# The second tile's M4, M7 and M3 go by quarter blocks, on one core

## The chip, the core and the metric

The kernel runs on one core of a Trainium2 chip. The metric is the device time of one execution in microseconds, and less is better. Five engines of the core matter here: TensorE (PE), whose weight loads are listed apart as PEld, VectorE (DVE), ScalarE (ACT), GpSimd (POOL) and SyncE (SP), which only issues DMAs. Each works through its own instruction queue in the order in which it was written, and semaphores make one wait for another.

## The reference

```python
def _attn_ref(q, k, v, proj):              # 4 batches, 8 heads, 768 rows, 64 wide
    mask = q_bucket[:, :, :, None] == k_bucket[:, :, None, :]   # hash buckets from the signs of q@proj, k@proj
    scores = np.where(mask, scale * np.matmul(q, k.transpose(0, 1, 3, 2)), -1e9)
    ...
    return np.matmul(attn, v)

def _moe_ref(x, w_in, w_out):              # x 3072 x 512, w_in 512 x 2048, w_out 2048 x 512
    h = x @ w_in
    sp = np.maximum(h, 0.0) + np.log1p(np.exp(-np.abs(h)))
    g = h * erf(sp)
    return (g @ w_out).astype(np.float32)
```

The attention's output, 3072 rows of 512, is the `x` of the feed-forward part. Everything is in float32. The change is in the feed-forward part alone.

## The kernel before

**The two halves.** Attention comes first and takes the span up to about 312 us. `feed_forward` (from L1341 on) then works on six tiles of 512 rows each, t = 0 to 5.

**Two products of a tile.** A tile's first product, `x @ w_in`, and its second, `g @ w_out`, are each done by Strassen's scheme in the form of Winograd: a 2 x 2 block product costs seven block products (M1 to M7, and P1 to P7 on the first side) in place of eight, and sums of blocks in between. For tiles 1 to 5 the first side goes two levels deep: each of the seven P is again seven quarter products Q1 to Q7 (`small`, L1672), 49 in all, called the chain of the tile. A quarter product is four matmuls of 128 rows by 128 columns. The profile shows a float32 matmul as two records, so a chain has 392.

**The second side** takes the gated hidden values in four quarters a11, a21, a12, a22 (`quarter`). `presum_g` (L1908) makes the sums S.0 (s1 = a21 + a22), S.1 (s2 = s1 - a11), S.2 and S.3 of them on DVE, each in two halves fl = 0, 1. M6 multiplies s2 and M5 s1; M1, M2, M3, M4 and M7 multiply quarters. A block product done whole (`project`, L1989) is eight products of two matmuls of 256 columns: 16 matmuls, 32 records. Done by quarter blocks (`project_small`, L2145) it is seven quarter products of four matmuls of 128 columns: 28 matmuls, 56 records. That form needs four sums of its left operand on DVE (`presum_a`, L2120, words A4.0 to A4.3 for M4), and three sums of its weights, which POOL makes with four instructions (`presum_b`, L2069). The sums of weights lie in one buffer, key `("b",)`, part of it in a slot of the ring of chain weights. The first tile that uses them also writes them to DRAM (`keep_b`, L2079, POOL), and every later tile loads them from there (`load_b`, L2083, SP). Four ACT copies (L2158) and two DVE adds (L2163, L2167) take the results out of PSUM; `combine` (L2030 and L2032) joins the seven products.

**Slots.** While PE does the chain of tile t + 1, it also does the second side of tile t; the two are interleaved product by product. Below, slot n is the stretch in which the chain of tile n runs. In slot 1, tile 0's second side is done, in slot 2 tile 1's, and so on; tile 5's comes behind slot 5. `script(t)` (L1913) writes down the order of tile t's second side in words. Tile 0 has a script of its own, tile 1 (`t < HALVES`) goes through all seven products whole, and tiles 2 to 4 mix: M6 with the pieces of M4, M5 with those of M7, and then M3 in pieces. Tile 5 mixes M2 with M4 and M6 with M7, and does M3 whole.

**Gating.** Between the two sides stands the gate, for each quarter in two halves: six ACT passes over 128 x 1024 (L1821, L1829 four times, L1846) and three DVE passes (L1835 twice, L1850).

**The order.** Each piece of work is an `op` with an engine, an assumed cost, what it reads and writes, and a rank. `by_need` (L187) plays the whole feed-forward part with these costs several times, and the order that it finds is the order in which the instructions are written into the queues. On PE the lowest rank goes first among what is ready by the plan, on the other engines what is due first. A chain's product has rank t + (place / 49). A second-side product has rank `at` + (place / 56), with `at` = t + 1 + LAG, so LAG says by how much the second side stands behind the chain. The ring of chain weights has two places: `load_wi` (L1641, on SP) loads the weights of one P, 1792 KB, as soon as the P before the last has been done.

Of the kernel before, what the change touches and what calls it, by code (L numbers as in the profile page):

```python
# [294 lines left out]
def kernel(  # L295
# [34 lines left out]
    small = ctx.enter_context(tc.tile_pool(name="small", bufs=3))  # L330
# [1010 lines left out]
    def feed_forward(pools, check, late):  # L1341
        again = late is None
        work = pools["work"]
        NTILE = NT // T
# [24 lines left out]
        def op(name, engine, cost, rank, fn, args, reads=(), writes=(), after=(), **more):  # L1369

            needs = set(after)
            for x in tuple(reads) + tuple(writes):
                if x in wrote:
                    needs.add(wrote[x])
            for x in writes:
                needs |= read.get(x, set())
            for x in reads:
                read.setdefault(x, set()).add(name)
            for x in writes:
                wrote[x] = name  # L1380
                read[x] = set()
            needs.discard(name)
            more.setdefault("late", dict(PE=0.4, DVE=0.3, ACT=0.3, POOL=0.35, SP=0.3)[engine])
            ops.append(
                Op(name, engine, cost, rank, lambda: fn(*args), after=tuple(sorted(needs, key=str)), **more)
            )
# [526 lines left out]
        def script(t):  # L1913
            if t == 0 and not again:
                first = " ".join(f"{name}.{k}" for ks in (range(4), range(4, 8)) for name in ("M1", "M2", "M4") for k in ks)
                return first + " C.0 C.1 C.4 S.0 S.1 S.2 S.3 M6 C.2 M7 C.3 C.9 M5 C.5 M3 C.7"
            if t < HALVES and not again:
                return "M1 C.11 S.0 S.1 S.2 M2 C.12 S.3 M4 C.4 M6 C.2 M7 C.3 C.9 M5 C.5 M3 C.7"
# [35 lines left out]
            )  # L1954


        HALVES = 2

        OPERAND = dict(M1=0, M2=2, M3=2, M4=3, M5="s1", M6="s2", M7=1)

# [205 lines left out]
            u = into_of(name)[:, 1, :]  # L2166
            nc.vector.tensor_tensor(out=u, in0=flat(bank_of(t, "Z" + name[1]))[:, P:TH], in1=u, op=ALU.add)  # L2167

        LAG, LAST_LAG = 0.04, 0.16

        def second_ops(t):

            at = t + 1 + (LAG if t != NTILE - 2 else LAST_LAG)

            def presums(k, rank):
                for fl in range(2):
# [62 lines left out]
            def whole(name):  # L2239
                return tuple(("wt", WHOLE_KEY[name], fl) for fl in range(2)) if name in WHOLE_KEY else (("w22",),)  # L2240

            def blocks_of(name):
                if t == HALVES and not again:
                    for k in range(4):
                        op(
                            ("presum_b", name, k),
                            "POOL",
                            1.26,
                            (1, at + 0.1, k),
                            presum_b,  # L2250
                            (name, k),
                            port=True,
                            reads=whole(name),
                            writes=(("b",), ("w", "P4", 0), ("w", "P4", 1)) + (whole(name) if k == 0 else ()),
                        )
                    op(
                        ("keep_b", name),
                        "POOL",
                        1.5,
                        (1, at + 0.1, 4),  # L2260
                        keep_b,
                        (name,),
                        reads=(("b",),),
                        writes=(("mb", name),),
                        late=5.0,
                        far=True,
                    )
                    return

                apart = name == "M4" and t < NTILE - 1  # L2270
                op(
                    ("load_b", t, name),
                    "SP",
                    0.1,
                    (1, at + now[0] / 56, 0),
                    load_b,
                    (name,),
                    reads=(("mb", name),),
                    writes=(("b",),),
                    after=(("small", t + 1, 0, "Q4"),) if apart else (),  # L2280
                    late=7.0,
                    far=True,
                )
# [58 lines left out]
            def take_word(word):  # L2342
# [6 lines left out]
                elif kind == "N1":  # L2349
                    now[0] += 0.5  # L2350
                    products("M1", int(rest), t + 1)
                    now[0] += 0.5
                elif kind == "S":
                    k = int(rest)
                    presums(k, (0.05, 0.1, 0.2, 0.4)[k])
                elif kind == "C":
                    combines(int(rest))
                elif kind[0] == "L":
                    blocks_of("M" + kind[1])
                elif kind == "T":  # L2360
                    op(
                        ("turn", t),
                        "POOL",
                        1.26,
                        (1, at + 0.1),
                        presum_b,
                        ("M3", 0),
                        port=True,
                        writes=(("w22",),),
                    )  # L2370
                elif kind[0] == "A":
                    sums("M" + kind[1], int(rest))
                elif kind[0] == "R":
                    take("M" + kind[1], rest)
                else:
                    now[0] += 0.5
                    half(kind, rest)
                    now[0] += 0.5
# [50 lines left out]
        for t in range(1, NTILE + 1):  # L2429
            rest = second_ops(t - 1)  # L2430
            if t < NTILE:
                x_ops(t)
                chain_ops(t)
                for q in (0, 2, 3, 1):
                    gate_ops(t, q)
            rest()
        if late:
            for k, (engine, cost, name) in enumerate(
# [9 lines left out]
                    after=((name, k // 2), ("late", k - 1)),  # L2448
# [66 lines left out]
    with ExitStack() as rooms:  # L2515
        with tc.manual_schedule():
            late = attention()
            pools = open_pools(rooms)
            ending = feed_forward(pools, (measured, judge, decide, ask), late)
        with tc.If(bound["again"] == 0, preferred_fallthrough_block=False) as arms:  # L2520
            with tc.manual_schedule():
                for each in ending:
                    each.emit()
        with arms.Else():
            general(pools)
            feed_forward(pools, None, None)
# [53 lines left out]
```

## Time and profile before

| | |
|---|---|
| Time, median of 3 runs (lowest to highest) | 874.19 us (872.89 to 875.64) |
| The profiled execution | 874.26 us, of which 872.5 us are its span |
| Chains of tiles 1 to 5 begin at | 364.9, 454.5, 546.6, 638.5 and 728.9 us; the last ends at 813.6 |
| Weight sums on POOL (L2069) | M4's begin at 498.7, M7's at 590.0, M3's at 614.3 us |
| Tile 1's M1, M2, M4, M6, M7, M5 and M3 begin at | 458.9, 473.0, 485.2, 498.4, 512.5, 524.7 and 538.8 us |
| M6 of tile 2 and the first piece of its M4 begin at | 577.4 and 579.1 us |

Times within the span are counted from its first instruction. The page gives busy time for each engine. Since matmuls are pipelined, the time from the start of one record to the start of the next says more of PE's rate than the mean duration of one does. A wait is shown in square brackets behind an instruction: how long its engine sat idle before it, and whose semaphore came last.

### The profile page before, as it was taken

How to read it: one execution, taken by the hardware profiler on the slowest of the kernel's cores; microseconds unless marked ns; L12 is line 12 of the kernel's file. 1: busy time of each engine (PE TensorE's matmuls, PEld its weight loads, DVE VectorE, ACT ScalarE, POOL GpSimd, SP SyncE). 2: the span in 40 equal slices, each digit the busy share in tenths (PEclk: the TensorE clock that was granted, in tenths of full speed). 3: DMA queues.
4: the chain of work that ended last, by engine and by line, in shares of the span. 5: the costliest groups of instructions: out<-in, count | busy, mean ns of one | idle time of the engine just before them, and what ended most of it. 6: DMA issues, size and time to landing. Idle time of an engine off the chain costs nothing.

```text
span 872.5 us, 15270 instructions
## 1 busy us (share of the span) xinstructions
PE 864.5 (99%) x5992; PEld 670.8 (77%) x5992; DVE 748.8 (86%) x926; ACT 638.2 (73%) x895; POOL 209.8 (24%) x274
## 2 busy tenths in 40 slices
PE   9999999999999999999999999999999999999997
PEld 5444544444454468998999999999999999999996
DVE  5999999999899799789996877799779978898982
ACT  6888888888888757786589467845777586758840
POOL 1112121111111000425241453235732433110000
PEclk9999999999999999999999999999999999999999
DMA  9567766556662255685564647555586657655211
GB/s 228 149 190 194 222 187 182 171 150 172 181 177 96 87 173 204 234 315 188 192 182 145 229 154 209 179 168 184 146 271 224 206 158 219 215 177 162 98 61 41
DMA packets 99825, 155.30 MB, mean 178 GB/s; under 512 B 35182, under 2 KB 48542, under 8 KB 98848
## 3 DMA queue, kind: packets, MB, share of 16 engines
q1 hardware_dynamic: 90112, 120.96, 44.8%
q0 software_dynamic: 9184, 32.81, 12.3%
q8 instruction: 49, 0.80, 0.4%
q10 hardware_dynamic: 448, 0.46, 0.2%
q14 instruction: 32, 0.26, 0.1%
HBM read 119.50 MB, written 29.46 MB: 171 GB/s over the span
## 4 chain that ended last, share of the span: by engine, by line
PE 94%; DMA 3%; DVE 1%; issue 1%; ACT 1%; DVEq 0%
PE M L1672 23%; PE M L1989 22%; PE st L687 18%; PE av L772 14%; PE M L1433 6%; PE M L2145 5%; DMA w_in_sb<-wi_P 3%; PE X L2145 2%; PE bits L975 1%; PE bits L816 1%; PE warm L936 1%; DVE area L1908 0%; PE X L1989 0%; DVE h L1850 0%; DVE e L1835 0%
## 5 line engine op out<-in xcount | busy, mean ns | idle before, releaser
L687 PE MATMUL st<-q,k 64*128 64x384 f32 x768 | 155.1, 483 | 0.0
L1672 PE MATMUL M<-area,w_in_sb 128*128 128x128 f32 x1120 | 146.7, 275 | 1.8 <-DVE h L1702 1.2
L1672 PEld LDWEIGHTS M<-area,w_in_sb 128*128 128x128 f32 x1120 | 142.2, 192 | 6.9 <-DVE h L1702 1.6
L1835 DVE SCALAR_TENSOR_TENSOR e<-w,e 128x1024 f32<-128x1024 f32 x96 | 125.0, 1302 | 20.0 <-ACT w L1829 19.5
L1702 DVE TENSOR_TENSOR h<-M,h 128x512 f32<-128x512 f32 x161 | 108.4, 686 | 33.5 <-PE M L1672 29.7
L1989 PE MATMUL M<-w_out_sb,h 128*128 128x256 f32 x528 | 130.8, 380 | 1.7 <-issue 1.7
L1829 ACT ACTIVATE w<-h,cq 128x1024 f32<-128x1024 f32 x96 | 109.7, 1142 | 22.0 <-DVE e L1835 22.0
L1829 ACT ACTIVATE w<-w,cq 128x1024 f32<-128x1024 f32 x96 | 110.3, 1149 | 1.8
L1672 PEld LDWEIGHTS M<-i,w_in_sb 128*128 128x128 f32 x840 | 107.9, 192 | 3.9
L1672 PE MATMUL M<-i,w_in_sb 128*128 128x128 f32 x840 | 110.4, 275 | 0.0
L1989 PEld LDWEIGHTS M<-w_out_sb,h 128*128 128x128 f32 x528 | 92.8, 191 | 10.5 <-issue 2.0
L1989 PE MATMUL M<-wt,area 128*128 128x256 f32 x384 | 96.3, 380 | 0.0
L687 PEld LDWEIGHTS st<-q,k 64*128 64x128 f32 x768 | 68.5, 187 | 35.7 <-issue 34.4
L760 DVE TENSOR_TENSOR area<-area 128x1536 f32<-128x1536 f32 (+1 forms) x46 | 79.2, 1721 | 6.9 <-ACT area L714 5.7
L1654 POOL TENSOR_TENSOR i<-area,i 128x128 f32<-128x128 f32 x70 | 46.3, 681 | 139.6 <-PE M L1672 138.6
L1821 ACT ACTIVATE e<-h,cq 128x1024 f32<-128x1024 f32 x48 | 54.9, 1144 | 33.8 <-DVE h L1702 22.0
L714 ACT ACTIVATE e_even<-st 128x768 f32<-128x768 f32 x96 | 73.9, 820 | 0.4 <-PE st L687 0.3
L714 ACT ACTIVATE area<-st 128x768 f32<-128x768 f32 x90 | 72.7, 811 | 0.3 <-PE st L687 0.3
L1989 PEld LDWEIGHTS M<-wt,area 128*128 128x128 f32 x384 | 66.9, 191 | 6.0 <-DVE area L1908 0.2
L1850 DVE TENSOR_TENSOR h<-h,e 128x1024 f32<-128x1024 f32 x48 | 61.0, 1271 | 9.8 <-ACT e L1846 9.8
L772 PE MATMUL av<-e_even,v 128*64 128x385 f32 x384 | 65.7, 490 | 0.0
L687 PE MATMUL st<-both 64*128 64x384 bf16 x384 | 63.0, 323 | 0.2 <-ACT e_even L714 0.2
(187 smaller groups left out, 1323.9 us busy)
## 6 DMA issues: line engine op xcount, KB each, us to landing
w_in_sb<-wi_P SPq DMA_DIRECT2D x35, 1792.0 KB
raw<-in_w_out_dram POOLq DMA_DIRECT2D x16, 512.0 KB, 4.1
raw<-in_w_in_dram POOLq DMA_DIRECT2D x14, 512.0 KB, 5.5
v<-in_v_dram SPq DMA_DIRECT2D x32, 192.0 KB
out_dram<-area SPq DMA_DIRECT2D x23, 256.0 KB
q<-in_qkT_dram SPq DMA_DIRECT2D x30, 192.0 KB
k<-in_qkT_dram SPq DMA_DIRECT2D x30, 192.0 KB
r<-rd SPq DMA_DIRECT2D x30, 192.0 KB
```

What stands on the lines that cost most here:

```text
L687: nc.tensor.matmul(out=st[:, ab, 0:HS], lhsT=d["k" + src][rows, keys], rhs=d["q" + src][rows, cols], start=(part == 0), stop=(part == 1),)
L714: nc.scalar.activation(out=e[:, :, 0:HS], in_=st[:, :, 0:HS], func=AF.Exp, scale=scale)
L760: nc.vector.tensor_tensor(out=into, in0=one, in1=two, op=ALU.add)
L772: nc.tensor.matmul(out=d["av", half][rows, 0:w], lhsT=d["v"][:, g * GC + c, rows], rhs=e[:, ab, 0:w], start=(g == 0 and c == 0), stop=(g = ...
L1672: nc.tensor.matmul(out=out_[:, c, :], lhsT=ring[:, W_AT[q], n % 2, c * P : (c + 1) * P], rhs=x, start=((q in ("Q1", "Q5") or q == "Q2" and ...
L1702: nc.vector.tensor_tensor(out=out_, in0=bank_, in1=one, op=ALU.add)
L1821: nc.scalar.activation(out=s, in_=unit(t, q, fl), func=AF.Sigmoid, bias=cq[:, 0:1])
L1829: nc.scalar.activation(out=st["q", t, q, fl, j], in_=f, func=func, scale=scale, bias=cq[:, column : column + 1])
L1835: nc.vector.scalar_tensor_tensor(out=s, in0=st.pop(("q", t, q, fl, j)), scalar=GATE_S[j][1], in1=s, op0=ALU.add, op1=ALU.mult,)
L1850: nc.vector.tensor_tensor(out=h, in0=h, in1=st.pop(("s", t, q, fl)), op=ALU.mult)
L1989: nc.tensor.matmul(out=where[:, sub, :], lhsT=a[:, j // G, j % G, sub * P : (sub + 1) * P], rhs=b[:, j, :], start=first, stop=end, skip_gr ...
L2145: nc.tensor.matmul(out=where[:, n * P : n * P + P], lhsT=a[:, j, :], rhs=b[:, j, :], start=(q in ("Q1", "Q2") and j == 0), stop=(q in ("Q4 ...
```

## The change

`HALVES` falls from 2 to 1, so tile 1 is no longer done whole: it takes the mixed script of tiles 2 to 4, and M4, M7 and M3 of tile 1 go by quarter blocks. `blocks_of` tests `t == HALVES`, so the weight sums of M4, M7 and M3 are now made and kept in the slot of tile 1's second side, and tile 2 loads them from DRAM, as tiles 3 to 5 do. The sums get one more wait: none of them is made before the first quarter product of the next tile's chain (`("small", t + 1, 0, "Q1")`). Two ranks are moved: the second side of tile 0 stands behind its chain by 0.05 and no longer 0.04, that of tile 4 by 0.13 and no longer 0.16.

```diff
-        HALVES = 2
+        HALVES = 1
...
-        LAG, LAST_LAG = 0.04, 0.16
+        LAG, LAST_LAG = 0.04, 0.13
...
-            at = t + 1 + (LAG if t != NTILE - 2 else LAST_LAG)
+            at = t + 1 + (0.05 if not t else LAG if t != NTILE - 2 else LAST_LAG)
...
                             (name, k),
                             port=True,
                             reads=whole(name),
+                            after=(("small", t + 1, 0, "Q1"),),
                             writes=(("b",), ("w", "P4", 0), ("w", "P4", 1)) + (whole(name) if k == 0 else ()),
```

## The prediction

> **What bounds the kernel now.** I read the page's first two parts and its chain first.
>
> ```profile
> PE 864.5 (99%) x5992; PEld 670.8 (77%) x5992; DVE 748.8 (86%) x926; ACT 638.2 (73%) x895; POOL 209.8 (24%) x274
> ...
> PEclk9999999999999999999999999999999999999999
> ...
> PE 94%; DMA 3%; DVE 1%; issue 1%; ACT 1%; DVEq 0%
> ```
>
> PE is busy throughout, at the full granted clock, and 94% of the chain that ended last is PE. Then I read the windows, cut so that each of the first five holds the 392 records of one chain: slots 1 to 5 and what is behind them.
>
> ```profile
> core 0: us, PE busy (x) PEld busy (x) DVE busy (x) ACT busy (x) POOL busy (x), PEclk, DMA share, GB/s
> 364.90:454.50 89.60, 88.40 (x597) 82.61 (x597) 79.74 (x86) 67.77 (x73) 35.72 (x43) 1.00 0.67 227
> 454.50:546.60 92.10, 92.10 (x617) 86.34 (x616) 70.36 (x73) 63.78 (x72) 34.07 (x41) 1.00 0.57 183
> 546.60:638.50 91.90, 91.90 (x697) 88.37 (x697) 75.59 (x85) 58.15 (x73) 43.39 (x47) 1.00 0.57 181
> 638.50:728.90 90.40, 90.34 (x690) 86.86 (x688) 79.24 (x94) 64.67 (x80) 30.16 (x33) 1.00 0.64 209
> 728.90:813.60 84.70, 84.21 (x632) 80.72 (x633) 72.38 (x88) 65.94 (x78) 12.83 (x20) 1.00 0.58 184
> ```
>
> In slot 2, where the change acts, PE is never idle. So a microsecond less of PE work there is a microsecond less of time, as long as no wait takes its place. The waits of PE that there are stand in its timeline; these three hold nearly all of its idle time behind the first chain's start:
>
> ```profile
> 410.29 1.16 PE L1672 MATMUL M<-area,w_in_sb 128*128 128x128 f32 x8 [1.20 <-DVE h L1702]
> 740.23 1.16 PE L1672 MATMUL M<-area,w_in_sb 128*128 128x128 f32 x8 [0.45 <-DMA w_in_sb<-wi_P]
> 861.88 3.69 PE L1989 MATMUL M<-w_out_sb,h 128*128 128x256 f32 x16 [1.66 <-issue]
> ```
>
> The last is the branch ahead of tile 5's M3, which stays.
>
> **The products.** The price of both forms comes from starts, since matmuls overlap. Whole (from the chain of waits, eight records, in alternation with chain products as in slot 2) and by quarters (PE's timeline, the first and the last of ten rows, all of L1672 or L2145 with 128 columns, 88 records between the two starts):
>
> ```profile
> 742.28 1.73 PE M L1989 x8
> 744.01 1.78 PE M L1672 x16
> ```
>
> ```profile
> 717.07 1.06 PE L2145 MATMUL M<-w_out_sb,h 128*128 128x128 f32 x8
> ...
> 726.89 1.06 PE L2145 MATMUL X<-w_out_sb,h 128*128 128x128 f32 x8
> ```
>
> Whole: 1.73 / 8 = 0.216 us a record, times 32 = 6.92 us. By quarters: (726.89 - 717.07) / 88 = 0.1116, times 56 = 6.25 us. One block product falls by 0.67 us and three by **2.0 us**, with 0.05 either way for rounding. Slot 4, which has three block products by quarters, is 90.4 us against 92.1 for slot 2: 1.7, which fits, as the slots are not cut at the same place of the second side.
>
> **What DVE gets in slot 2.** The rows are those of slot 3, where tile 2 already goes by quarters (DVE busy in L2120, L2163, L2167, then L2032 in slots 2 and 4):
>
> ```profile
> 546.60:638.50 91.90, 11.26 (x12) 1.00 0.57 181
> ...
> 546.60:638.50 91.90, 1.25 (x3) 1.00 0.57 181
> ...
> 638.50:728.90 90.40, 0.85 (x3) 1.00 0.64 209
> ...
> 454.50:546.60 92.10, 2.07 (x3) 1.00 0.57 183
> 638.50:728.90 90.40, 5.61 (x7) 1.00 0.64 209
> ```
>
> Twelve sums of operands cost 11.3 us and six adds out of PSUM 1.25 + 0.85 = 2.1. `combine` has five adds in the mixed script (C.13, C.9, C.5, C.6, C.14) and had three: two more of 5.61 / 7 = 0.8, that is 1.6. Together 15.0 us, so DVE in slot 2 goes from 70.4 to about 85.4 of 90.1 us: 95%. Slot 1 has 79.7 of 89.6 (89%) and the one PE wait on DVE; slot 4 has 79.2 of 90.4 (88%) and none. So I cost these 15 us at nothing, hidden by PE's 90, but this cover is thin; a rival below says what it costs when it gives out.
>
> **POOL and DMA.** Of the twelve weight sums, M4's four are in slot 2 already (498.7). M7's and M3's eight move there from slot 3:
>
> ```profile
> 546.60:638.50 91.90, 13.89 (x8) 1.00 0.57 181
> ```
>
> POOL (L2069 in slot 3) gets 13.9 us more in slot 2, 34.1 to 48 of 90, and as much less in slot 3. M7's sums can only overwrite the buffer when M4's pieces have been read; POOL stands still meanwhile, and the chain's own small sums (L1654) and x sums (L453) are queued behind. In slot 3 this happened and PE, the one who waits for them, did not stand:
>
> ```profile
> 591.35 2.14 POOL L2069 TENSOR_TENSOR w_in_sb<-w_out_sb 128x512 f32<-128x512 f32 x1
> 597.14 1.28 POOL L2069 TENSOR_TENSOR w_in_sb<-w_out_sb,w_in_sb 128x512 f32<-128x512 f32 x1 [3.66 <-PE M L2145]
> ```
>
> The same distances hold in slot 2: cost nothing. The new wait, for Q1 of the next chain, ends a microsecond into slot 2; M4's sums need 4 x 13.89 / 8 = 7 us, and M4's third piece, their first reader, comes after 485: nothing. Tile 2 loads its weight sums with six more DMAs on SP. Slots 4 and 5 carry the same loads, and there a load of chain weights was late only where SP had issued it late, behind an output:
>
> ```profile
> 729.40 0.39 SPq L2038 DMA_DIRECT2D out_dram<-area  x1
> 729.88 0.52 SPq L1641 DMA_DIRECT2D w_in_sb<-wi_P  x1
> ```
>
> That load is the 0.45 us wait at 740.23, 10.3 us after its issue. A seventh of slot 2, the time that a load has there, is 13 us. Since tile 1's outputs will bunch at the end of slot 2 as tile 3's do here, the same could happen at slot 3's start; there M products fill the time, so I take nothing, with 0.5 as the upper end. ACT gets twelve small copies and loses two large ones, about +2 us on 63.8 of 90, on nobody's path.
>
> **What comes earlier.** M4's place is taken by M6, mixed with M4's pieces. So M6, which needs the sum S.1, starts where M4 starts now, 485.24, and not at 498.4. Here is who makes S.1 (its first half; ACT's saturate, then DVE's gate, S.0, a PSUM add, S.1):
>
> ```profile
> 478.41 1.04 ACT L1846 ACTIVATE e<-e 128x1024 f32<-128x1024 f32 x1
> 479.80 1.06 ACT L1846 ACTIVATE e<-e 128x1024 f32<-128x1024 f32 x1 [0.34 <-DVE e L1835]
> ```
>
> ```profile
> 480.78 1.45 DVE L1850 TENSOR_TENSOR h<-h,e 128x1024 f32<-128x1024 f32 x1
> 482.27 1.23 DVE L1908 TENSOR_TENSOR area<-h,h 128x1024 f32<-128x1024 f32 x1
> 483.69 0.69 DVE L1702 TENSOR_TENSOR h<-M,h 128x512 f32<-128x512 f32 x1 [0.19 <-PE M L1672]
> 484.29 1.22 DVE L1908 TENSOR_TENSOR area<-area,h 128x1024 f32<-128x1024 f32 x1
> ```
>
> ```profile
> 485.24 1.03 PE L1989 MATMUL M<-wt,h 128*128 128x256 f32 x4
> ```
>
> S.1's first half ends at 485.51, 0.3 us after M6 could start. In slot 3 it was ready at 561.44, 16 us ahead of M6 at 577.4:
>
> ```profile
> 560.07 1.37 DVE L1908 TENSOR_TENSOR area<-area,h 128x1024 f32<-128x1024 f32 x1
> ```
>
> So this is the tightest new step. DVE has room ahead: without the add between, and with the gate right behind the saturate that ends at 479.45, three passes of 1.23 end near 483.3, 1.9 us early. The planner gives S.1 an earlier due time with the new order, so it should do some of this. Bounds: a stall from 0 to about 2 us; I take 0.3, the row as it stands.
>
> **The ranks.** Tile 0 behind by 0.01 more, about half a product: the order around 405 us barely changes by rank (one chain product passes M4's last, and so the PSUM add that PE waits for at 410.29 can start up to 0.9 us sooner). Bounds: nothing, to the 1.2 us of that wait; also a loss of as much, as the whole order is played anew. I take 0.3 gained. Tile 4 ahead by 0.03 (1.7 places, 1.5 us of PE work): slot 5's chain ends later, and so tile 5's gates start later. Behind the chain's end ACT is full of gates, its longest wait for them the first row; the tightest reader is M5's fifth product, 16 records behind the start at 839.99, at 843.45, for S.0's second half, ready at 842.61:
>
> ```profile
> 814.20 1.15 ACT L1829 ACTIVATE w<-h,cq 128x1024 f32<-128x1024 f32 x1 [1.06 <-DVE e L1835]
> ```
>
> ```profile
> 841.38 1.23 DVE L1908 TENSOR_TENSOR area<-h,h 128x1024 f32<-128x1024 f32 x1
> ```
>
> ```profile
> 839.99 7.93 PE L1989 MATMUL M<-wt,area 128*128 128x256 f32 x36
> ```
>
> With 0.84 us of slack and ACT's backlog ahead: nothing, at most 1.5 - 0.84 = 0.7 lost.
>
> **The sum**: 2.0 for the products, 0.3 lost at M6, 0.3 gained at 410. The profiled execution took 874.26, 872.5 of span and 1.8 around it; 872.3 for the same execution, and against the median of 874.19, lower by 0.07, **872.2 us**, 0.23% faster. That is within what a measurement of this kernel tells from no change, about 0.3% or 2.6 us.
>
> [...] DVE and POOL slow each other here: S.2 of tile 2 took 2.30 us beside POOL's x sums, S.3 2.12 beside the weight sums (L1908 alone: 1.22).
>
> ```profile
> 584.62 2.30 DVE L1908 TENSOR_TENSOR h<-h,h 128x1024 f32<-128x1024 f32 x1
> ...
> 590.24 2.12 DVE L1908 TENSOR_TENSOR h<-h,area 128x1024 f32<-128x1024 f32 x1
> ```
>
> So one collision costs DVE about 1.08 us, and eight more of them in slot 2 would cost 8.6: 94 of 90.1, the third rival. In slot 3 the eight sums averaged 13.89 / 8 = 1.74, against 1.28 alone, so POOL pays part of it.
>
> [...]
>
> **The rivals.**
> 1. *The stall at 410 goes as well* (and perhaps the one at 740): for it speaks that only one PSUM add was late; against it that M6 and its neighbours keep their order by rank. 0.9 more of the 1.2 at 410 and the 0.45 at 740: 872.2 - 1.4 = **870.8**. Chance 0.30.
> 2. *The last gates of tile 5 come late*: the 0.7 above is paid in full: **872.9**. Chance 0.05.
> 3. *Slot 2's DVE fills up.* Added to 85.4 us are up to 8.6 of blocking; of the 3.9 that exceed 90.1 I let half show as waits of PE on PSUM adds (1 to 3 us), and the gain is eaten: 872.2 + 2.0 = **874.2**. Against it speaks that gates can slide into slot 3, which loses the same blocking. Chance 0.20.
> 4. *Slower: M4's sums get ahead of S.1.* If DVE does the four operand sums of M4 (0.94 each in slot 3) before tile 1's last gate and S.1, and POOL's weight sums block two of the passes by 1.07, S.1 ends at 485.5 + 3.8 + 2.1 = 491.4, and M6 and all behind it stand 6.2 us: 872.2 - 0.3 + 6.2 = **878.1**. From 2.3 us of this stall the change loses, measurably from 4.9. The due times speak against it. Chance 0.07.
>
> The forecast has the rest, 0.38, with a range of its own of 871.2 to 873.2. That the change doesn't do what it says cannot be: the script fixes the products.
>
> **How the numbers follow.** Faster by over 0.3% means below 871.6: nearly all of rival 1 (0.29) and the lower quarter of the forecast (0.10): 0.39. Slower by over 0.3%, above 876.8: rival 4 and the tail of rival 3: 0.09. The rest, 0.52, is within 0.3%. The range from 870.3 to 875.0 leaves out rival 4, the upper part of 3 and the lowest of 1.
>
> **What would show it.** Right: 168 more records of L2145 and 96 fewer of L1989 in slot 2, the stretch from slot 2's start to slot 3's start shorter by about 2 us, weight sums of all three in slot 2, and no PE wait there over 0.5 us. M6's first record near 485 with a wait on DVE L1908 would show the tight step; PE waits on DVE L1702 through slot 2 rival 3; a wait of some microseconds on L1908 rival 4; no wait at 410 rival 1. I am wrong if PE's record spacing in slot 2 differs from 0.216 and 0.112, or if the replayed order opens a wait in a slot that I left untouched.

## The result, and the profile after

| | before | after |
|---|---|---|
| Time, median of 6 runs each (lowest to highest) | 874.22 us (872.89 to 875.64) | 878.47 us (877.73 to 879.28) |
| Ratio, with its 95% interval | | 1.0051 (1.0041 to 1.0062) |
| Profiled execution, its span | 874.26, 872.5 us | 879.28, 877.5 us |

The change makes the kernel slower by 0.51%, 4.3 us, where 872.2 was forecast. The page of after has these rows:

```profile
PE 866.6 (99%) x6064; PEld 673.6 (77%) x6064; DVE 762.1 (87%) x946; ACT 640.2 (73%) x905; POOL 214.6 (24%) x274
...
PEclk9999999999999999999999999999999999999998
...
q8 instruction: 50, 0.82, 0.4%
...
PE 95%; DMA 2%; DVE 1%; ACT 1%; issue 1%; DVEq 0%
```

PE has the 72 more records that the scripts ask for (3 x 56 in place of 3 x 32), and 72 more weight loads: 144 more instructions. Block products by quarters take less time than whole ones (6.25 us against 6.92, by the prediction's spacing of records), and still PE is busy for 2.1 us longer. The second row has the reason: in the last fortieth of the span the granted clock is no longer full (0.84 from 855.5 us to the end). The chain of waits is still nearly all PE.

So I cut the span where PE's last product ahead of the branch of tile 5's M3 ends, and took one window from the start of the chain of tile 1 up to there, of before and then of after. The columns are those of the windows in the prediction: length, then busy time of PE, PEld, DVE, ACT and POOL.

```profile
364.90:860.06 495.16, 493.41 (x3525) 467.82 (x3524) 413.69 (x463) 343.29 (x404) 158.24 (x182) 1.00 0.57 184
```

```profile
365.70:860.11 494.41, 491.74 (x3597) 468.33 (x3595) 426.82 (x483) 345.20 (x414) 163.08 (x182) 1.00 0.57 189
```

Up to the branch the two kernels take the same time: it is reached at 860.06 and at 860.11. PE's work in this stretch fell by 1.7 us, and its idle time rose from 1.75 to 2.67. **All of the 5.0 us that the span grew lies behind the branch**: 872.5 - 860.06 = 12.4 us before, 877.5 - 860.11 = 17.4 after. PE's timeline there, of after (start, duration, then the wait in brackets; the row of before is the third of the waits in the prediction):

```profile
859.24 1.03 PE L1989 MATMUL M<-wt,area 128*128 128x256 f32 x4
861.37 0.67 PE L1989 MATMUL M<-w_out_sb,h 128*128 128x256 f32 x2 [1.09 <-issue]
864.44 6.04 PE L1989 MATMUL M<-w_out_sb,h 128*128 128x256 f32 x14 [2.41 <-issue]
870.32 3.62 PE L1989 MATMUL X<-w_out_sb,h 128*128 128x256 f32 x16
```

And the windows of the same end:

```profile
859.30:863.40 4.10, 1.64 (x7) 1.00 (x7) 1.68 (x3) 0.58 (x1) 0.00 (x0) 1.00 0.05 13
863.40:870.30 6.90, 5.86 (x14) 4.62 (x14) 1.29 (x2) 0.00 (x0) 0.00 (x0) 0.51 0.24 80
870.30:877.00 6.70, 3.64 (x17) 2.85 (x15) 0.85 (x2) 0.00 (x0) 0.00 (x0) 1.00 0.12 39
```

M3 of tile 5 began with two records, stood for another 2.41 us with nothing in the profile to wait for, and then its other 14 records went at half the clock (0.51): 870.32 - 864.44 = 5.88 us, 0.42 a record in place of 0.216. The sum: the second wait costs 864.44 - 861.37 - 2 x 0.216 = 2.6 us, the half clock 5.88 - 14 x 0.216 = 2.9, and from the end of the last product to the branch's first record it is 861.37 - 860.11 = 1.3 us, 0.6 less than before (861.88 - 860.06). That is 4.9, all but 0.1 of the growth.

In just that second wait the DMA view of after (861.4 to 864.4 us) shows a packet of the queue that carries instructions:

```profile
q8 instruction: 1, 0.02, 2.2%
```

By the page all 50 of its packets have 0.82 MB, so one has 16.4 KB: by the queue's name, a piece of some engine's code. That made the theory. The packet alone proves nothing: in before such a packet also runs behind the branch's first record (863.02 to 864.00 us), and no second wait goes with it.

### The profile page after: what moved, and what is told of

Same layout as the page of the kernel before. It is cut to its first block, busy times and chain, and to the rows that moved or that the text cites. A ratio compares the mean times of both kernels' runs of the same rounds, so it can differ in the third digit from the quotient of the medians.

```text
span 877.5 us, 15442 instructions
## 1 busy us (share of the span) xinstructions
PE 866.6 (99%) x6064; PEld 673.6 (77%) x6064; DVE 762.1 (87%) x946; ACT 640.2 (73%) x905; POOL 214.6 (24%) x274
## 4 chain that ended last, share of the span: by engine, by line
PE 95%; DMA 2%; DVE 1%; ACT 1%; issue 1%; DVEq 0%
PE M L1672 24%; PE M L1989 21%; PE st L687 18%; PE av L772 14%; PE M L1433 6%; PE M L2145 6%; PE X L2145 3%; DMA w_in_sb<-wi_P 2%; PE bits L975 1%; PE bits L816 1%; ACT w L1829 1%; PE warm L936 1%; PE X L1989 0%; DVE h L1850 0%; DVE area L1908 0%
## 5 line engine op out<-in xcount | busy, mean ns | idle before, releaser
L1989 PE MATMUL M<-w_out_sb,h 128*128 128x256 f32 x464 | 118.6, 387 | 3.5 <-issue 3.5
L1989 PEld LDWEIGHTS M<-w_out_sb,h 128*128 128x128 f32 x464 | 83.0, 195 | 12.2 <-issue 4.1
L1654 POOL TENSOR_TENSOR i<-area,i 128x128 f32<-128x128 f32 x70 | 50.9, 746 | 139.5 <-PE M L1672 138.5
L2158 ACT COPY area<-M 128x128 f32<-128x128 f32 x56 | 14.6, 261 | 67.1 <-PE M L2145 66.8
```

What stands on the lines that cost most here:

```text
L1989: nc.tensor.matmul(out=where[:, sub, :], lhsT=a[:, j // G, j % G, sub * P : (sub + 1) * P], rhs=b[:, j, :], start=first, stop=end, skip_gr ...
```

## The experiments

**Theory A, the code's place.** The products and all up to the branch do as forecast or a little worse. The time is lost because 144 more PE instructions push the code behind the branch to where a cut between two pieces of code falls right behind the branch's target. **Theory B, the order.** The two ranks or the new loads open waits in the feed-forward part, and these delay the end. The first set tells these apart. To move the code without touching the work, matmuls that are never carried out are put at the head of the branch's other arm (taken only when the scores are too large); its code lies ahead of that of the arm that is taken.

**e1: the changed kernel, its code 64 PE instructions further on** (16 dead matmuls are 32 records and 32 weight loads).

```diff
         with arms.Else():
+            for _ in range(16):
+                nc.tensor.matmul(out=bank("dead")[0:D, 0:D], lhsT=ones, rhs=ones, start=True, stop=True)
             general(pools)
```

> The changed kernel with 16 matmuls added at the head of the branch that is not taken, which are never executed; only the place of TensorE's code behind them moves, by 64 instructions. Theory A (the second wait behind the branch, 2.4 us, and the half clock of 6.8 us after it come from where the taken branch's code lies, so that TensorE must fetch another 16 KB piece a few instructions in): the second wait and the half clock go, 5.0 us, 878.5 to about 873.5. Theory B (they come from the work ahead of the branch, which the change altered): no difference, 878.5.

Measured: 873.95 us (872.79 to 874.58), 1.0002 of before (0.9992 to 1.0012), span 871.6. PE's timeline at the end of e1:

```profile
858.31 1.03 PE L1989 MATMUL M<-wt,area 128*128 128x256 f32 x4
860.94 3.69 PE L1989 MATMUL M<-w_out_sb,h 128*128 128x256 f32 x16 [1.61 <-issue]
864.47 3.62 PE L1989 MATMUL X<-w_out_sb,h 128*128 128x256 f32 x16
```

The second wait is gone, the 16 records go as one, 3.53 us from their start to the next product's or 0.22 each, and the clock stays full (1.000 over the span). What follows: 1.0051 - 1.0002 = 0.49%, 4.3 us, come from the place of the code alone. But what is left is no gain: the work as changed is worth nothing against before.

**e2: the kernel before, with its code moved by the same 144 instructions** (36 dead matmuls).

```diff
         with arms.Else():
+            for _ in range(36):
+                nc.tensor.matmul(out=bank("dead")[0:D, 0:D], lhsT=ones, rhs=ones, start=True, stop=True)
             general(pools)
```

> The kernel before with 36 matmuls added in the branch that is not taken, never executed, so that the taken branch's code lies at the very place that it has in the changed kernel. Theory A: the second wait and the half clock come up in a kernel that has none of the change, about 874.2 + 5.0 = 879.2. Theory B: 874.2 as before.

Measured: 878.34 us (877.79 to 879.54), 1.0055 (1.0038 to 1.0072), span 876.1. PE's timeline of e2, and a window in it:

```profile
860.85 0.67 PE L1989 MATMUL M<-w_out_sb,h 128*128 128x256 f32 x2 [1.33 <-issue]
864.32 4.87 PE L1989 MATMUL M<-w_out_sb,h 128*128 128x256 f32 x14 [2.80 <-issue]
869.03 3.62 PE L1989 MATMUL X<-w_out_sb,h 128*128 128x256 f32 x16
```

```profile
865.30:868.70 3.40, 3.40 (x10) 2.69 (x9) 0.00 (x0) 0.00 (x0) 0.00 (x0) 0.50 0.26 84
```

What follows: the kernel before, with none of the change in what it does, gets the same time as after, the same second wait behind two records, and half a clock. That the place of the code makes the loss is shown from both sides.

**e8: the kernel before, its code 12 instructions less far than in e2** (33 dead matmuls), so that the cut comes six records later.

```diff
+            for _ in range(33):
+                nc.tensor.matmul(out=bank("dead")[0:D, 0:D], lhsT=ones, rhs=ones, start=True, stop=True)
```

> The kernel before with 33 matmuls in the branch not taken, so that the taken branch's code begins 12 instructions earlier against the fetched pieces than in the second run, which stood after 6. Theory A: TensorE does some 18 instructions first, the second wait comes later in the branch and shrinks by 12 x 0.108 = 1.3 us, from 2.96 to about 1.7 us: 878.3 - 1.3 = 877 or less, down to 875 if the clock no longer halves. Rival (a fetch that is independent of the place inside the piece): 878.3 as in the second run, or 873.7 as before.

Measured: 875.68 us, 1.0025 (1.0015 to 1.0034), span 873.2. PE's timeline of e8:

```profile
861.11 1.97 PE L1989 MATMUL M<-w_out_sb,h 128*128 128x256 f32 x8 [1.09 <-issue]
864.38 1.89 PE L1989 MATMUL M<-w_out_sb,h 128*128 128x256 f32 x8 [1.30 <-issue]
866.10 3.62 PE L1989 MATMUL X<-w_out_sb,h 128*128 128x256 f32 x16
```

The wait moved just as the cut did, from behind two records to behind eight. And from the first record of the branch to the first behind the cut it is 3.07 us in after, 3.47 in e2 and 3.27 here: about the same whatever lies between. So the records ahead of the cut are cover for something that takes some 3.3 us from the branch's first record on. The packets in the three traces say what: one of 16.4 KB on the queue that carries instructions ends at 863.02 us in after, at 862.89 in e2 and at 862.99 here, and PE goes on 1.42, 1.43 and 1.39 us behind its end. That ties the wait to a fetch of code. With six more records the wait is shorter by 1.5 us, and the clock stays full (1.000 over the span, 0.215 us a record behind the cut).

**e3: the changed kernel with the two ranks of before**, its code moved as in e1.

```diff
-        LAG, LAST_LAG = 0.04, 0.13
+        LAG, LAST_LAG = 0.04, 0.16
...
-            at = t + 1 + (0.05 if not t else LAG if t != NTILE - 2 else LAST_LAG)
+            at = t + 1 + (0.04 if not t else LAG if t != NTILE - 2 else LAST_LAG)
```

> The changed kernel with the two ranks put back to 0.04 and 0.16, code moved as in the first run. Under theory A the end is clean. If the two ranks are worth what the prediction took for them (0.3 us at 410 and nothing at tile 5), it lies within 0.5 us of the first run, near 873.5; if the ranks are what kept the body from falling by 2 us, it is at 872.2 or below; if they helped, the wait at 740 is back and it is at 874 or above.

Measured: 871.43 us (870.83 to 872.38), 0.9975 (0.9965 to 0.9984), span 869.4. This is the best version of the study, faster than both kernels. Its window from the start of the first chain to the branch:

```profile
365.05:857.05 492.00, 491.27 (x3597) 468.14 (x3595) 425.96 (x483) 344.16 (x414) 167.75 (x182) 1.00 0.58 190
```

PE is idle for 492.00 - 491.27 = 0.73 us there, in e1 for 2.40. What follows: the ranks, not the quarter blocks, took back what the quarter blocks gained. To place this, one rank was put back at a time, all with the old value of the other and the code moved as in e1.

**e5: 0.05 for tile 0, 0.16 for tile 4. e6: 0.04 and 0.13. e10: 0.03 and 0.16.**

```diff
 # e5
-        LAG, LAST_LAG = 0.04, 0.13
+        LAG, LAST_LAG = 0.04, 0.16
 # e6
-            at = t + 1 + (0.05 if not t else LAG if t != NTILE - 2 else LAST_LAG)
+            at = t + 1 + (0.04 if not t else LAG if t != NTILE - 2 else LAST_LAG)
 # e10: both, with 0.03 in the place of 0.04
```

> The changed kernel with only tile 4's rank put back (0.16), tile 0's left at 0.05; code moved as in the first run. Theory D (tile 0's rank cost the 2.5 us between the first and the third run: its waits at 406 and 410, and the later start of slot 2's last load behind the accumulating DMA, which makes the wait at 548): about 873.4, the waits at 406 and 548 there, none at 835. Theory E (tile 4's rank cost it): about 871.4.

> The changed kernel with only tile 0's rank put back (0.04), tile 4's left at 0.13; code moved. Theory D: about 871.7, no wait at 548, at most the 0.3 us at 835. Theory E: about 873.9.

> The third run's kernel with tile 0's rank at 0.03, the other way from the change, code moved. If the time goes steadily with that rank (0.05: 873.9, 0.04: 871.4), it is below 871.4, near 870.5. If a rank only deals the order anew, it lies anywhere between 871 and 874, with waits of PE at other places than in the third run.

Measured, each ratio against before on the same chip (its medians beside these runs were 873.68 us for e1 and e3, 873.49 for e5 and e6, 873.56 for e10), with the stretch from the first chain's start to the branch and PE's idle time in it (length less PE's busy time of one window each, as above):

| kernel | time, us | ratio (95%) | stretch, us | PE idle, us |
|---|---|---|---|---|
| before | 874.22 | 1 | 495.16 | 1.75 |
| e1 (0.05, 0.13) | 873.95 | 1.0002 (0.9992 to 1.0012) | 494.13 | 2.40 |
| e3 (0.04, 0.16) | 871.43 | 0.9975 (0.9965 to 0.9984) | 492.00 | 0.73 |
| e5 (0.05, 0.16) | 873.89 | 1.0004 (0.9994 to 1.0014) | 494.38 | 2.59 |
| e6 (0.04, 0.13) | 872.79 | 0.9989 (0.9979 to 0.9999) | 493.73 | 2.04 |
| e10 (0.03, 0.16) | 873.85 | 1.0001 (0.9991 to 1.0010) | 494.26 | 2.87 |

Either rank alone costs: 0.05 some 2.5 us against e3, 0.13 some 1.3; the two together 2.5, so they don't add. The second of these is barely clear of noise, since the intervals of e3 and e6 just overlap, but PE's idle time agrees (2.04 against 0.73 us). That 0.03 costs as much as 0.05 says that there is no right side of 0.04 to be on, but an order that happens to fit: the low 0.73 of e3 is luck in the same sense. One wait of each kernel's PE timeline, in the order e5, e6, e10:

```profile
824.95 1.16 PE L2145 MATMUL X<-w_out_sb,h 128*128 128x128 f32 x8 [0.42 <-DVE area L2163]
```

```profile
823.47 1.16 PE L2145 MATMUL X<-w_out_sb,h 128*128 128x128 f32 x8 [1.02 <-DVE area L2163]
```

```profile
406.19 1.10 PE L1989 MATMUL M<-wt,area 128*128 128x256 f32 x4 [1.60 <-ACT e L1846]
```

A rank of tile 0 opens a wait in tile 4's second side, 420 us later, which e3 doesn't have. The row of e5 is the smallest of its four waits; the others are 0.56 us at 406.84, 0.75 at 411.28 and 0.86 at 548.58, and the four make up its 2.59. In e6 the rest is 1.01 at 410.07, in e10 0.76 at 548.55 and 0.42 at 824.92. So e5 came out as theory D had it, with one more wait, and e6 between the two theories: tile 4's rank costs as well. Why each value deals just these waits stays open.

**e4: the changed kernel; M3's weight sums are stored only behind the start of the next chain**, code moved as in e1. After has a wait that before hadn't, at 549, where tile 1's outputs end; PE's timeline, then SP's, then POOL's, of after:

```profile
549.02 1.16 PE L1672 MATMUL M<-area,w_in_sb 128*128 128x128 f32 x8 [1.38 <-DMA w_in_sb<-wi_P]
```

```profile
534.30 13.89 SPq L1641 DMA_DIRECT2D w_in_sb<-wi_P  x2
```

```profile
534.26 0.87 POOL L1709 DMA_DIRECT2D h<-area  x1
...
541.08 0.86 POOL L2079 DMA_DIRECT2D wm_M<-w_in_sb  x1
541.62 0.87 POOL L2079 DMA_DIRECT2D wm_M<-b  x1
```

The first of the two loads of chain weights in the SP row, issued at 534.30, is there only at 549. Beside it run an accumulating DMA, issued in the same microsecond, and the stores of M3's weight sums, which the change brought into this slot. e4 takes the stores away from it:

```diff
+                        after=(("small", t + 2, 0, "Q1"),) if name == "M3" else (),
```

> The changed kernel, code moved as in the first run, with the store of M3's weight sums to DRAM held back until the first quarter product of tile 3's chain. Theory C (TensorE's wait of 1.4 us for chain weights at 549 comes from that store, 768 KB in the same microseconds as that load and the two accumulating DMAs): the wait goes, 1.4 to 1.6 us below the first run, about 872. Rival (the load is late for the other traffic, or waits for its issue): the wait stays and the time is that of the first run.

Measured: 873.51 us, 0.9991 (0.9979 to 1.0003), against e1's 1.0002 (0.9992 to 1.0012). The wait at that place, in e1 and then in e4:

```profile
548.08 1.16 PE L1672 MATMUL M<-area,w_in_sb 128*128 128x128 f32 x8 [1.05 <-DMA w_in_sb<-wi_P]
```

```profile
547.91 1.16 PE L1672 MATMUL M<-area,w_in_sb 128*128 128x128 f32 x8 [0.49 <-DMA w_in_sb<-wi_P]
```

Without the stores the wait is half as long as in e1, but it didn't go, where theory C had it go. How much of it is the stores' isn't settled, since other kernels that have them there wait 0.76 us (e10) to 1.38 (after). The time doesn't tell e1 and e4 apart: in e4 a wait of 0.81 us on ACT at 406.55 stands where e1 has one of 0.49 on DVE. In e3, e6 and e9, with the same stores, there is no wait: there the accumulating DMA goes out a microsecond ahead of the load (531.83 and 532.80 in e3). In after, e1, e4, e5, e7 and e10 it goes out within 0.05 us of the load, and all six have the wait. That this is its cause is argued from that; the accumulating DMA was not moved by itself.

**e7: e3 without the new wait for the next chain's Q1.**

```diff
-                            after=(("small", t + 1, 0, "Q1"),),
```

> The third run's kernel (both old ranks) without the new wait for Q1 of the next chain. The prediction costed this wait at nothing: then the time is the third run's 871.4 within 0.7 us. If the wait is what keeps POOL from taking M4's sums into slot 1, where DVE is 96% busy, it is slower: each of four sums that blocks one DVE pass costs about 1.1 us of DVE in slot 1, 872.5 to 875.

Measured: 874.9 us, 1.0023 (1.0009 to 1.0037), span 873.1. Against e3's 0.9975, taking the wait away costs 0.48%, some 4 us. Without it M4's weight sums don't begin at 454.4, as in e3, but at 407.2. POOL's timeline of e7, then DVE's, then PE's:

```profile
407.19 2.25 POOL L2069 TENSOR_TENSOR wt<-wt 128x512 f32<-128x512 f32 x1
...
411.71 2.13 POOL L2069 TENSOR_TENSOR w_in_sb<-wt,w_in_sb 128x512 f32<-128x512 f32 x1
```

```profile
408.23 2.28 DVE L1908 TENSOR_TENSOR area<-h,h 128x1024 f32<-128x1024 f32 x1
...
411.04 1.69 DVE L1908 TENSOR_TENSOR area<-area,h 128x1024 f32<-128x1024 f32 x1
412.64 2.28 DVE L1908 TENSOR_TENSOR h<-h,h 128x1024 f32<-128x1024 f32 x1
```

```profile
411.17 1.16 PE L1672 MATMUL M<-area,w_in_sb 128*128 128x128 f32 x8 [1.51 <-DVE h L1702]
412.77 2.86 PE L1989 MATMUL M<-wt,area 128*128 128x256 f32 x12 [0.45 <-DVE area L1908]
...
549.65 0.60 PE L1672 MATMUL M<-area,w_in_sb 128*128 128x128 f32 x3 [1.15 <-DMA w_in_sb<-wi_P]
```

The weight sums fall beside S.0, S.1 and S.2 of tile 0, just where DVE's results are waited for (there DVE is busy nearly without a gap, though over the whole of slot 1 it is 91% busy in e3, not 96%). These passes take 2.28, 1.69 and 2.28 us, in e3 1.47, 1.21 and 1.21, and PE waits 1.51 + 0.45 us behind them, where e3 has 0.69. This is the collision of the prediction's third rival, in slot 1 and not in slot 2. It makes 1.3 us of PE's wait. In all PE is idle for 495.57 - 491.96 = 3.6 us up to the branch; nearly all of the rest is the load of chain weights at 549.65 and 0.43 us at 826.02, places at which e5 and e10 wait too. So part of the 4 us is an order dealt anew, as with the ranks. S.2's 2.28 is 1.07 over its 1.21 in e3, and POOL's own sums take up to 2.25 beside these passes, against 1.28 at 458.9 in e3, so here both sides lose.

**e9: e3 with its code not moved.** One question was left: does the best order lose to before too, as it is written?

> The third run's kernel (both old ranks) without the 16 matmuls in the branch not taken. The taken branch then begins about 4 instructions ahead of the cut between two fetched pieces (8 in the changed kernel). Theory A: it has the second wait and the half clock, 871.4 + 4.6 to 5.2 = 876.0 to 876.6, slower than before although its body is the fastest of all. Rival (the body's gain of the third run came with the added code in another way): 871.4 or anything but that.

Measured: 877.17 us (875.49 to 877.43), 1.0039 (1.0024 to 1.0054), span 875.4. PE's timeline of e9:

```profile
856.22 1.03 PE L1989 MATMUL M<-wt,area 128*128 128x256 f32 x4
861.98 6.39 PE L1989 MATMUL M<-w_out_sb,h 128*128 128x256 f32 x16 [4.73 <-issue]
```

The clock of e9 is the third number from the end of its window:

```profile
860.60:867.40 6.80, 5.42 (x13) 4.34 (x14) 1.29 (x2) 0.00 (x0) 0.00 (x0) 0.50 0.22 70
```

Here no record lies between the branch and the cut, where some 4 instructions were expected, and both waits are one of 4.73 us; the packet of 16.4 KB ends at 860.52, 1.46 us before PE goes on. Then the clock is halved as in after. So with the quarter blocks, the best order is 0.25% faster than before or 0.39% slower, by where the code behind one branch happens to lie.

## Why the prediction was wrong

**The branch, "which stays": the step that failed.** The prediction saw the wait ahead of tile 5's M3, priced it in the trace of before (1.66) and kept it, since the change does nothing there. But its length belongs to the place of the code, and the change adds 144 instructions ahead of it. Taken alone this costs 4.3 us (after against e1) or 4.8 (before against e2), the whole of the loss. Neither a rival nor the range had a term for it.

**The products: right.** The forecast was 2.0 us less. PE's busy time in the stretch up to the branch fell by 1.7 (after) and by 2.1 (e3), with exactly the 72 more records. The stretch from slot 2's start to slot 3's start did not get shorter, as I had said it would: 92.1 became 94.3. The windows show that the boundary moved as well: 701 records lie in it, where 617 + 72 = 689 would.

**The ranks: the term was mis-sized.** I took 0.3 gained at 410, nothing for tile 4, and bounds of 1.2 and 0.7 for a loss. Together they lose 2.5 us (e1 against e3), 0.05 alone 2.5 and 0.13 alone 1.3. The wait at 410 split in two and hardly shrank in all; PE's timeline of after, and then of e3:

```profile
406.77 3.69 PE L1989 MATMUL M<-wt,area 128*128 128x256 f32 x16 [0.43 <-DVE area L1908]
...
411.20 1.16 PE L1672 MATMUL M<-area,w_in_sb 128*128 128x128 f32 x8 [0.74 <-DVE h L1702]
```

```profile
409.86 1.16 PE L1672 MATMUL M<-area,w_in_sb 128*128 128x128 f32 x8 [0.69 <-DVE h L1702]
```

Most of the gain that rival 1 hoped for is there in e3, without the new ranks: 0.69 in place of 1.20, and the wait at 740 is gone. I had written that "the whole order is played anew", but took my bounds from the two places next to the tiles whose ranks change, as if the rest stayed.

**The chain weights at slot 3's start: mis-sized.** "Nothing", with 0.5 as the upper end; it is 1.38 in after and 1.05 in e1, nothing in e3. I looked for a load issued late behind outputs. It was issued in time and landed late: PE had it only 14.7 us behind its issue.

**DVE in slot 2, POOL's sums, the Q1 wait: right in time, for a reason that I had not named.** The windows of slot 2 of after, first of all work and then of the operand sums (L2120) and the weight sums (L2069) alone:

```profile
454.70:549.00 94.30, 92.94 (x701) 89.12 (x700) 82.23 (x88) 61.55 (x76) 53.98 (x54) 1.00 0.58 190
...
454.70:549.00 94.30, 11.36 (x12) 1.00 0.58 190
...
454.70:549.00 94.30, 22.14 (x12) 1.00 0.58 190
```

DVE has 82.2 of 94.3 us, not 85.4 of 90.1, since three of `combine`'s five adds slid into slot 3; no wait of PE on DVE is seen in slot 2. The twelve weight sums take 22.1 us there, and PE waits for none of them. The wait for Q1 delays nothing that is seen, as forecast, but it is no mere safety: without it 4 us are lost (e7).

**M6 and S.1: 0.3 taken, nothing lost.** DVE's timeline of after and then PE's:

```profile
472.21 1.22 DVE L1908 TENSOR_TENSOR area<-area,h 128x1024 f32<-128x1024 f32 x1
```

```profile
486.32 1.03 PE L1989 MATMUL M<-wt,area 128*128 128x256 f32 x4
```

S.1's first half is done at 473.4, 13 us before M6, with no wait there: the due time moved it, as the prediction thought it might. So rival 4, whose 878.1 us is nearly what was measured, comes near it by luck and is false in its mechanism: M4's sums never stand in S.1's way.

**The sum, as it should have been.** From 872.5 of span: 2.1 less by the products and 1.0 less by PE's waits up to the branch, so e3's 869.4. Then 2.2 for the two ranks (e1: 871.6), of which 1.7 are PE's waits, and 5.0 for the code's place. That makes 876.6. The remaining 0.9 is mostly the start of the first chain, at 365.70 in this execution of after and at 365.04 in e1, whose order is the same. By medians the gain of e3 is 2.2 us (1.4 to 3.1 by the interval), less than the spans' 3.1: the profiled execution of before, 874.26, lies above the median of before beside e3, 873.68, and that of e3, 871.22, below its own.

## What to carry to other kernels

Where a kernel branches late, measure a change that adds or removes instructions ahead of the branch with the code moved, too, before a verdict on the change itself: here the place of the code alone cost 4.3 us (after against e1, 64 instructions apart) and 4.8 (e2 against before, 144 apart), with no work there changed. Judge a change and its re-tuned ranks apart, since a rank replays the whole order and its price need not lie beside the tile that it names. And a wait that seems needless may keep work out of a place where it would collide (here taking it away cost some 4 us, 1.3 of them by the collision), so take it away once and see.

## What the runs showed of the hardware

**Code came in packets of 16.4 KB, and behind this branch PE waited for one.** The page of after has 50 packets with 0.82 MB on the queue that carries instructions. With the cut 2 or 8 records behind the branch's target (after, e2, e8), PE has the next piece 3.07 to 3.47 us behind the first record of the target. What work lies between is the cover: behind two records the wait is still 2.41 and 2.80 us, behind eight 1.30. A cut right at the target costs 4.73 us in one (e9). In these four traces PE goes on 1.39 to 1.46 us behind the end of a packet of 16.4 KB. By this, an estimate from these runs, a cut 16 records (3.5 us) behind the target would cost nothing; that was not tried. The branch's own wait (1.66 us in before, 1.61 in e1, with no cut near) looks like such a fetch too, since the branch's first record comes 1.60 us behind the end of a packet of 16.4 KB in before and 1.53 in after; no run takes that packet away.

**Behind these waits the clock was at half.** Waits of 1.09 and 2.41 us with two records between them went with 6.9 us at 0.51 of the clock (after), of 1.33 and 2.80 with 3.4 us at 0.50 (e2); 1.09 and 1.30 with eight records between them left it full, at 1.000 over the span (e8). One wait of 4.73 went with 6.8 us at 0.50 (e9). After and e2, with nearly the same waits, lose 2.9 and 1.7 us to it (14 records in 5.88 and in 4.71 us). What sets how long the clock stays at half, and where the limit lies between waits that bring it down and waits that don't, no run shows.
